# Channel mixing: the two groups of the first batch take turns feature by feature, in an order written out by hand

## The chip, the cores and the metric

The kernel runs on one core of one Trainium2 chip. TensorE does matrix products into PSUM (eight banks of 2 KB per partition), VectorE (DVE) and ScalarE (ACT) do the vector work, GpSimd (POOL) a little of it, SyncE (SP) issues the DMAs. The metric is the device time of one execution in microseconds.

## The reference, cut to what matters

Three layers follow each other on 4 batches of 768 positions and 384 channels.

```python
def _attn_ref(q, k, v, beta):                 # a recurrence over 768 positions, 4 batches x 8 heads
    ...
    return y                                  # gives x [4, 768, 384]

def _moe_ref(x, w_ch1, w_ch2):                # w_ch1 [384, 1536], w_ch2 [1536, 384]
    X = np.fft.fft(x, axis=1)
    X = np.fft.fft(X, axis=2)
    u = x + np.real(X)
    mu = np.mean(u, axis=-1, keepdims=True)
    var = np.mean((u - mu) ** 2, axis=-1, keepdims=True)
    un = (u - mu) / np.sqrt(var + 1e-06)
    return u + np.maximum(un @ w_ch1, 0.0) @ w_ch2

def _moe2_ref(x, w_in, w_spatial, b_spatial, w_out):
    ...                                       # a second mixer, over positions and channels
```

The change lies in `_moe_ref`, which is called channel mixing below.

## The kernel before

The recurrence is worked in chunks of 64 positions, batch by batch, and ends at about 316 us of the trace. While its last chunks run, batch 0 gets its Fourier transform and the normalised input of its first half is prepared. What follows is channel mixing, until 668 us, and then the second mixer.

**Groups and features.** Mixing takes the 3072 positions in eight groups of 384 (`for g in range(NG)`), two to a batch. The hidden layer of 1536 is cut into twelve features of 128. For a feature the first layer is nine products of 384 columns into one PSUM bank (L759: three chunks of the input times three passes, because each fp32 operand is split into a high and a low part). ScalarE takes the relu of that bank as the high part `hh` (L764), VectorE forms the low part `hl` (L765). The second layer is nine products into three accumulator banks `acc` (L774), which stay open over all twelve features; it runs one feature behind the first layer. At a group's end VectorE adds the three accumulators to x (L783).

**What stands beside the products.** Each of the 24 weight pieces (twelve of w_ch1, twelve of w_ch2) comes from DRAM as 8-byte numbers and is converted on the chip by `conv2`: one ScalarE pass (L677), three VectorE passes (L679, L680, L683), then the high part on ScalarE (L689) and the low part, the residual, on VectorE (L690). The first five pieces are converted ahead of mixing; the other 19 fall into it. The Fourier transform of batches 1 to 3 is `dft`: three vector steps on the rows (L575 to L586), one that combines them (L591 to L596), four first-stage pieces on TensorE (L603 to L609, copied out by L615), three second-stage pieces (L625, with L634 to L636) and an end that adds into x (L641 to L647). `mlp1_prep` prepares a group's input: statistics and reciprocal roots (L726 to L711), the normalised rows `un` (L731), and three chunks of three transposes each (L739), split into `uh` on ScalarE and `ul` on VectorE (L715, L716). Group 2 is the first of batch 1 and needs that batch's whole transform.

**Order and banks.** The recurrence is chained: `chain` makes each instruction stand behind the one before it on its engine, in the order of the code. In group 0 of mixing `behind` only keeps the instructions behind the recurrence; otherwise a scheduler, with a time model of its own, sets the order in mixing. Within the code `aside` hands out, one call a feature, conversions (in pairs), then transform steps, then the conversions of the last stage's weights. One PSUM pool holds the whole kernel: four X banks (first layer, transforms, transposes), three Y banks (accumulators) and one Z bank.

Of the kernel before, what the change touches and what calls it, by code (L numbers as in the profile page):

```python
# [33 lines left out]
PASS = ((0, 0), (0, 1), (1, 0))  # L34
# [4 lines left out]

CF = dict(
    skew=4, ring=20, kq=5, qt=3, mb=2, cvd=3, cve=2, kn=4, sv="hhhhhd", few=3,
    warm=20, keep=1, last=8, cuts=(0.5, 0.65), dfs=(1, 1, 1, 1, 2, 2, 3, 1, 1, 1, 2), cvt=(0, 0, 0, 0, 1, 1, 1, 1, 1, 1, 1), early=5, ahead=1,
)

BANKS = dict(X=4, Y=3, Z=1)
BANKS.update(pa="X", pz="Z", pb="Y", pc="Y", pd="Y", pf="X", h="X", o="Y", t="X")

# [6 lines left out]
WORD = [0] + [n for f in range(11) for n in (2 * f + 2, 2 * f + 1)] + [23]  # L56


class Kernel:
# [19 lines left out]
    def behind(self):  # L79
# [6 lines left out]
                self.tc.add_manual_dep(ins, last, dep, reason="issue order")  # L86
        self.seen = len(new)

    def load(self, out, in_):
        return self.nc.sync.dma_start(out=out, in_=in_)  # L90

    def bank(self, what, shape):
        tag = BANKS[what]
        t = self.ps.tile([128, 512], F32, name="bank" + tag, bufs=BANKS[tag])
# [472 lines left out]


    def dft(self, b, x, p):
        nc, sc, dc, sg = self.nc, self.sc, self.dc, self.sg  # L570
        X = x[b]
        ff = p(0, [128, 3, 388])
        for t in range(3):
            xs = p(3, [128, 2, DM])
            nc.vector.tensor_add(xs[:, 0], X[:, t], X[:, 3 + t])  # L575
            nc.vector.tensor_sub(xs[:, 1], X[:, t], X[:, 3 + t])
            f = p(6, [128, DM])
            nc.vector.tensor_copy(out=f[:, 0:193:192], in_=xs[:, 0, 0:193:192])
            nc.vector.tensor_add(f[:, 1:192], xs[:, 0, 1:192], xs[:, 0, 383:192:-1])
            nc.vector.tensor_sub(f[:, 193:384], xs[:, 1, 1:192], xs[:, 1, 383:192:-1])  # L580
            h = ff[:, t]
# [9 lines left out]
        nc.vector.tensor_add(sm, e1, e2)  # L591
        nc.vector.tensor_sub(e1, e1, e2)
        nc.vector.tensor_add(e2, e0, sm)
        nc.vector.scalar_tensor_tensor(out=r3, in0=e0, scalar=sg[:, 0:1], in1=e1, op0=MUL, op1=SUB)
        nc.vector.scalar_tensor_tensor(out=c15, in0=e0, scalar=sg[:, 1:2], in1=e1, op0=MUL, op1=ADD)
        nc.vector.scalar_tensor_tensor(out=e0, in0=e0, scalar=2.0, in1=sm, op0=MUL, op1=SUB)  # L596
# [119 lines left out]
        self.nc.vector.tensor_sub(lo, src, hi.bitcast(F32))  # L716


    def mlp1_prep(self, g, x, p):
        nc = self.nc  # L720
        assert g // 2 in self.mixed
        X = x[g // 2][:, g % 2 * 3 : g % 2 * 3 + 3]
        st = p.tile([128, 3, 6], F32, name="st1", bufs=2)
        mv = p.tile([128, 3, 2], F32, name="mv1", bufs=2)
        for t in range(3):
            nc.vector.bn_stats(out=st[:, t], in_=X[:, t])  # L726
            nc.vector.bn_aggr(out=mv[:, t], in_=st[:, t])
        r = self.rstd(p, mv, 3, "l1")
        un = p.tile([128, 3, DM], F32, name="un")
# [4 lines left out]
        u = [p.tile([128, 3, DM], F32R, name="u" + s, bufs=2) for s in "hl"]  # L734
        yield u
        for c in range(3):
            pt = self.bank("t", [128, DM])
            for t in range(3):
                nc.tensor.transpose(pt[:, t * 128 : t * 128 + 128], un[:, t, c * 128 : c * 128 + 128], self.idn)  # L739
            self.split(u[0][:, c], u[1][:, c], pt)  # L740
            yield u

    def mlp1(self, x, w1, w2, p, pu, cur, aside):
        nc = self.nc
        NG = NT // 3
        for g in range(NG):
# [3 lines left out]
            hs = {}  # L750
            for f in range(13):
                next(aside, None)
                if g == 0:
                    self.behind()
                if f < 12:
                    ph = self.bank("h", [128, DM])
                    for c in range(3):
                        for j, (i, k) in enumerate(PASS):
                            nc.tensor.matmul(  # L759
                                ph, lhsT=w1[f][i][:, c * 128 : c * 128 + 128], rhs=cur[k][:, c], start=(c + j == 0), stop=(c == 2 and j == 2)  # L760
                            )
                    hh = p.tile([128, DM], F32R, name="hh", bufs=3)
                    hl = p.tile([128, DM], F32R, name="hl", bufs=3)
                    nc.scalar.activation(hh, ph, AF.Relu)  # L764
                    nc.vector.scalar_tensor_tensor(  # L765
                        out=hl, in0=ph, scalar=0.0, in1=hh.bitcast(F32), op0=MAX, op1=SUB
                    )
                    hs[f] = (hh, hl)
                if f > 0:
                    e = f - 1  # L770
                    hx = hs.pop(e)
                    for t in range(3):
                        for j, (i, k) in enumerate(PASS):
                            nc.tensor.matmul(  # L774
                                acc[t],
                                lhsT=hx[i][:, t * 128 : t * 128 + 128],
                                rhs=w2[e][k],
                                start=(e == 0 and j == 0),
                                stop=(e == 11 and j == 2),
                            )  # L780
                if f in (5, 7, 9, 11):
                    new = next(gen, new)
            add = lambda t, xt: nc.vector.tensor_add(xt, acc[t], xt)  # L783
            sums = [(add, t, x[g // 2][:, g % 2 * 3 + t]) for t in range(3)]
            if g + 1 < NG:
                for f, *args in sums:
                    f(*args)
                sums = []
            cur = new
        for _ in aside:  # L790
            pass
        return sums


    def mlp2_prep(self, X, p):
# [102 lines left out]
    def run(self):  # L898
        nc, a = self.nc, self.a
        self.mixed, self.sc = set(), None  # L900
        c0, p0 = self.pool("keep")
        cps = self.tc.tile_pool(name="ps", bufs=1, space=PSUM)
        self.ps = cps.__enter__()
# [6 lines left out]
        e = {}  # L910
# [88 lines left out]

        sums = self.mlp1(x, [w[WORD.index(2 * f)] for f in range(12)], [w[WORD.index(2 * f + 1)] for f in range(12)], pm, e["u"], e["u0"], aside())  # L1000
        cm.__exit__(None, None, None)
        e["cu"].__exit__(None, None, None)
        cn, pn = self.pool("mlp2")
# [10 lines left out]
        cps.__exit__(None, None, None)  # L1014
        c0.__exit__(None, None, None)


# [107 lines left out]
```

## Time and profile before

| | us |
|---|---|
| median of three runs | 937.28 (937.04 to 937.43) |
| the profiled execution | 936.92 |
| its span, first to last instruction | 935.1 |
| TensorE busy | 884.8 (95%) |
| VectorE busy | 579.9 (62%) |
| ScalarE busy | 405.3 (43%) |
| GpSimd busy | 70.3 (8%) |

A profile is one execution of the program. Spans on TensorE have modelled ends, since products run into each other; a stream of products is read by the distance of their starts. [...] The chain of work that ended last is TensorE's for 72% of the span and VectorE's for 20%.

### The profile page before, as it was taken

How to read it: one execution, taken by the hardware profiler on the slowest of the kernel's cores; microseconds unless marked ns; L12 is line 12 of the kernel's file. 1: busy time of each engine (PE TensorE's matmuls, PEld its weight loads, DVE VectorE, ACT ScalarE, POOL GpSimd, SP SyncE). 2: the span in 40 equal slices, each digit the busy share in tenths (PEclk: the TensorE clock that was granted, in tenths of full speed). 3: DMA queues.
4: the chain of work that ended last, by engine and by line, in shares of the span. 5: the costliest groups of instructions: out<-in, count | busy, mean ns of one | idle time of the engine just before them, and what ended most of it. 6: DMA issues, size and time to landing. Idle time of an engine off the chain costs nothing.

```text
span 935.1 us, 18282 instructions
## 1 busy us (share of the span) xinstructions
PE 884.8 (95%) x7232; PEld 842.7 (90%) x7232; DVE 579.9 (62%) x1748; ACT 405.3 (43%) x1030; POOL 70.3 (8%) x75
## 2 busy tenths in 40 slices
PE   7969899999899769989999999999999999999998
PEld 7658888998898649989999999999999999899898
DVE  5999999998875899567479331322372442533521
ACT  2367878898966436222225111111261342332421
POOL 2000000000000000000000000000032132132221
PEclk8988999999999889999999999999999999999999
DMA  9676567643362530000150000000120000000001
GB/s 237 178 173 160 147 189 194 184 117 87 79 183 78 194 128 1 1 1 1 41 164 1 1 1 1 1 1 18 33 70 26 26 1 26 27 1 26 26 1 52
DMA packets 51160, 67.13 MB, mean 72 GB/s; under 512 B 28897, under 2 KB 41410, under 8 KB 51074
## 3 DMA queue, kind: packets, MB, share of 16 engines
q1 hardware_dynamic: 51074, 65.96, 24.9%
q8 instruction: 57, 0.93, 0.4%
q14 instruction: 29, 0.24, 0.1%
HBM read 61.22 MB, written 4.72 MB: 71 GB/s over the span
## 4 chain that ended last, share of the span: by engine, by line
PE 72%; DVE 20%; ACT 5%; issue 2%; DMA 1%; POOL 0%; ACTq 0%; DVEq 0%; POOLq 0%
PE bankX L759 14%; PE bankY L774 14%; PE bankX L867 11%; PE bankX L853 5%; PE bankX L828 5%; PE bankY L887 5%; DVE tm L273 4%; DVE Ts L278 4%; PE bankY L383 2%; PE bankY L367 2%; PE bankY L396 2%; PE bankY L398 2%; PE bankX L609 2%; PE bankX L198 1%; DVE cw L384 1%
## 5 line engine op out<-in xcount | busy, mean ns | idle before, releaser
L759 PE MATMUL bankX<-uh,w 128*128 128x384 f32 x576 | 163.9, 347 | 8.3 <-ACT w L689 4.7
L774 PE MATMUL bankY<-w,hh 128*128 128x384 f32 x576 | 136.6, 343 | 1.8 <-DVE w L690 1.5
L765 DVE SCALAR_TENSOR_TENSOR hl<-bankX,hh 128x384 fp32r<-128x384 f32 x96 | 52.7, 552 | 133.6 <-ACT hh L764 124.9
L764 ACT ACTIVATE hh<-bankX 128x384 fp32r<-128x384 f32 x96 | 46.8, 491 | 200.9 <-PE bankX L759 192.2
L759 PEld LDWEIGHTS bankX<-uh,w 128*128 128x128 f32 x576 | 106.5, 191 | 12.1 <-ACT w L689 6.4
L774 PEld LDWEIGHTS bankY<-w,hh 128*128 128x128 f32 x576 | 103.6, 190 | 4.2 <-DVE w L690 2.3
L867 PE MATMUL bankX<-ws,vh 128*128 128x384 f32 x384 | 98.9, 337 | 0.0
L759 PE MATMUL bankX<-ul,w 128*128 128x384 f32 x288 | 97.9, 340 | 0.0
L774 PE MATMUL bankY<-w,hl 128*128 128x384 f32 x288 | 82.2, 340 | 0.0
L875 DVE TENSOR_TENSOR g<-bankX,bsb 128x384 f32<-128x384 f32 x32 | 17.8, 558 | 103.6 <-PE bankX L867 103.6
L398 PE MATMUL bankY<-Sb,cw 112*112 112x96 f32 (+1 forms) x352 | 65.4, 269 | 11.4 <-DVE cw L384 9.2
L845 POOL TENSOR_TENSOR vl<-v,vh 128x512 fp32r<-128x512 f32 x24 | 31.7, 1328 | 531.0 <-DMA cvd<-in_ws_dram 457.4
L396 PE MATMUL bankY<-WU,gak 128*112 128x96 f32 (+1 forms) x384 | 69.3, 269 | 0.3
L867 PEld LDWEIGHTS bankX<-ws,vh 128*128 128x128 f32 x384 | 69.1, 188 | 0.0
L867 PE MATMUL bankX<-ws,vl 128*128 128x384 f32 x192 | 64.6, 337 | 0.0
L398 PEld LDWEIGHTS bankY<-Sb,cw 112*112 112x112 f32 (+1 forms) x352 | 49.1, 178 | 13.4 <-DVE cw L384 7.2
L278 DVE TENSOR_TENSOR Ts<-Ts,tm 128x110 f32<-128x110 f32 (+26 forms) x264 | 59.4, 263 | 0.8
L273 DVE TENSOR_TENSOR tm<-Ts 128x110 f32<-128x110 f32 (+26 forms) x264 | 59.3, 263 | 0.9
L367 PE MATMUL bankY<-gak,TT 128*128 128x96 f32 x384 | 53.4, 283 | 3.7 <-issue 2.7
L759 PEld LDWEIGHTS bankX<-ul,w 128*128 128x128 f32 x288 | 55.0, 191 | 0.0
L396 PEld LDWEIGHTS bankY<-WU,gak 128*112 128x112 f32 (+1 forms) x384 | 53.2, 181 | 1.2 <-ACT x L413 0.6
L774 PEld LDWEIGHTS bankY<-w,hl 128*128 128x128 f32 x288 | 53.2, 189 | 0.4 <-DVE hl L765 0.3
(166 smaller groups left out, 1787.3 us busy)
## 6 DMA issues: line engine op xcount, KB each, us to landing
kq<-in_kq_dram SPq DMA_DIRECT2D x40, 448.0 KB, 4.5
qt<-in_qt_dram SPq DMA_DIRECT2D x48, 196.0 KB, 3.8
gak<-in_kv_dram SPq DMA_DIRECT2D x48, 192.0 KB, 3.9
w<-in_w_dram SPq DMA_DIRECT2D x24, 384.0 KB, 7.0
out_dram<-ot SPq DMA_DIRECT2D x24, 192.0 KB, 2.0
kn<-in_kn_dram SPq DMA_DIRECT2D x16, 192.0 KB, 4.6
s<-in_wi_dram SPq DMA_DIRECT2D x6, 512.0 KB, 4.0
cvd<-in_ws_dram SPq DMA_DIRECT2D x12, 192.0 KB, 2.4
```

What stands on the lines that cost most here:

```text
L273: nc.vector.tensor_tensor(out=tm, in0=T[:, r, k : k + 1].to_broadcast(sh), in1=T[:, k : k + 1, :k].to_broadcast(sh), op=MUL)
L278: nc.vector.tensor_add(o, o, tm)
L367: nc.tensor.matmul(pb[:, hp].rearrange("p t d -> p (t d)"), lhsT=tt[:, o + hp], rhs=kv[:, hp], start=True, stop=True)
L396: nc.tensor.matmul(pd[:m, hp], lhsT=ak[:, hp, :m], rhs=u[:, hp], start=True, stop=(c == 0))
L398: nc.tensor.matmul(pd[:m, hp], lhsT=cw[:, hp, :m], rhs=sb[:, hp], start=False, stop=True)
L759: nc.tensor.matmul(ph, lhsT=w1[f][i][:, c * 128 : c * 128 + 128], rhs=cur[k][:, c], start=(c + j == 0), stop=(c == 2 and j == 2))
L764: nc.scalar.activation(hh, ph, AF.Relu)
L765: nc.vector.scalar_tensor_tensor(out=hl, in0=ph, scalar=0.0, in1=hh.bitcast(F32), op0=MAX, op1=SUB)
L774: nc.tensor.matmul(acc[t], lhsT=hx[i][:, t * 128 : t * 128 + 128], rhs=w2[e][k], start=(e == 0 and j == 0), stop=(e == 11 and j == 2),)
L828: nc.tensor.matmul(pv, lhsT=xT[t // 3][i][:, c, (t % 3) * 128 : (t % 3) * 128 + 128], rhs=wi[2 * c + 1][k], start=(c + j == 0), stop=(c == ...
L853: nc.tensor.matmul(pu, lhsT=wi[2 * c][i][:, f * 128 : f * 128 + 128], rhs=xT[hf][k][:, c], start=(c + j == 0), stop=(c == 2 and j == 2),)
L867: nc.tensor.matmul(pv, lhsT=vn[i][:, s, f * 128 : f * 128 + 128], rhs=ws[2 * s + hf][k], start=(s + j == 0), stop=(s == 5 and j == 2),)
```

## The change

Groups 0 and 1, the first batch, are worked together. A turn is one feature of one group: its first-layer products, what stands "between", then the second-layer products of that group's feature before. Group 0 starts, group 1 follows three features behind (`lag`), and then they alternate; turn n is counted through both groups: turns 0, 1 and 2 are group 0's features 0 to 2, turn 3 is group 1's feature 0, turn 4 group 0's feature 3 and so on to turn 25. Both groups read the same converted weights. For these turns the PSUM pool is closed and given out anew with two X banks, three Y and three V banks (group 1's accumulators), and afterwards again as before. Everything in these turns is chained in the order of the code: in each turn `beside` advances the last three weight conversions by one step each, and by tables `stats` and `turns` the preparation of groups 1 and 2 and the transform of batch 1 take their steps there. `dft` and `mlp1_prep` get places at which they can be split. From group 2 on the scheduler orders as before, and `aside` holds transforms 2 and 3 and then the last stage's weights. Group 1's `hh`, `hl` and group 2's input lie in another SBUF pool under the names `xh`, `xl`.

```diff
 CF = dict(
     ...
+    turns=(4, 5, 6, 7, 8, 9, 10, 11, 13, 14, 15, 16, 17, 17, 18, 19), stats=(((0, 1, 2, 3, 3), (2,)), ((20, 21, 22), (23, 24, 25))),
 )
 BANKS = dict(X=4, Y=3, Z=1)
+BANKS2 = dict(X=2, Y=3, V=3)
...
+    def psum(self, banks):
+        if self.ps:
+            self.cps.__exit__(None, None, None)
+        self.banks = banks
+        self.cps = self.tc.tile_pool(name="ps", bufs=1, space=PSUM, reuse_waits="tile")
+        self.ps = self.cps.__enter__()
...
-    def mlp1(self, x, w1, w2, p, pu, cur, aside):
+    def mlp1(self, x, w1, w2, p, pu, first, beside, aside):
...
+        def into(g, f, acc, cur, between=lambda: None):
+            if f < 12:
+                ph = self.bank("h", [128, DM])
+                ...
+                nc.scalar.activation(hh, ph, AF.Relu)
+                nc.vector.scalar_tensor_tensor(out=hl, in0=ph, scalar=0.0, in1=hh.bitcast(F32), op0=MAX, op1=SUB)
+                hs[g, f] = (hh, hl)
+            between()
+            if f > 0:
+                ...
+        self.psum(BANKS2)
+        accs = [[self.bank(n, [128, DM]) for _ in range(3)] for n in ("o", "o2")]
+        hx1 = [self.px.tile([128, 3, DM], F32R, name="x" + s, bufs=2) for s in "hl"]
+        lag, n = 3, 0
+        for s in range(13 + lag):
+            for g, f in ((1, s - lag), (0, s)):
+                if 0 <= f < 13:
+                    beside(n)
+                    into(g, f, accs[g], first[g], lambda: beside(n, True))
+                    if f == 12:
+                        for h, *args in sums(g, accs[g]):
+                            h(*args)
+                    self.chain()
+                    n += 1
+        self.psum(BANKS)
+        cur = first[2]
+        for g in range(2, NG):
...
+        def beside(n, between=False):
+            for g, (stats, turned) in enumerate(CF["stats"]):
+                for _ in range((turned if between else stats).count(n)):
+                    first[1 + g] = next(preps[g])
+            if between:
+                for _ in range(CF["turns"].count(n)):
+                    next(mx)
+                return
+            if len(gens) < 24 - CF["early"]:
+                gens.append(self.conv2(e["u"], w[CF["early"] + len(gens)]))
+            for g in gens[:-4:-1]:
+                next(g, None)
...
         def aside():
-            for i in range(CF["early"], 24):
-                self.conv(e["u"], w[i])
-                if i - CF["early"] >= CF["ahead"] and i % 2:
-                    yield
-            n = 0
-            while next(mx, 1) != 1:
-                n += 1
-                if not 4 < n <= 12 or n % 2 == 0:
+            for i, _ in enumerate(mx):
+                yield
+                if i % 12 < 4:
                     yield
```

Up to the first product of mixing the order on every engine is the same before and now, and in the second mixer too. Two places show what moves.

TensorE at the start of group 0, before: `uh` and `ul` are the parts of the normalised input, `w_F` the converted piece of feature F, `idn` the unit matrix of the transposes.

```order
L739 MATMUL bankX<-idn,un 128x128 x6
L759 MATMUL bankX<-uh,w_0_4306 128x384
L759 MATMUL bankX<-ul,w_0_4306 128x384
L759 MATMUL bankX<-uh,w_0_4306 128x384
L759 MATMUL bankX<-uh,w_1_4355 128x384
L759 MATMUL bankX<-ul,w_1_4355 128x384
L759 MATMUL bankX<-uh,w_1_4355 128x384
L759 MATMUL bankX<-uh,w_0_4306 128x384
L759 MATMUL bankX<-uh,w_1_4355 128x384
```

The same place now (the lines of the new file are 776 for the first layer, 792 for the second):

```order
L761 MATMUL bankX<-idn,un 128x128 x6
L776 MATMUL bankX<-uh,w_0_4306 128x384
L776 MATMUL bankX<-ul,w_0_4306 128x384
L776 MATMUL bankX<-uh,w_0_4306 128x384 x2
L776 MATMUL bankX<-ul,w_0_4306 128x384
L776 MATMUL bankX<-uh,w_0_4306 128x384 x2
L776 MATMUL bankX<-ul,w_0_4306 128x384
L776 MATMUL bankX<-uh,w_0_4306 128x384
L776 MATMUL bankX<-uh,w_1_4355 128x384
L776 MATMUL bankX<-ul,w_1_4355 128x384
L776 MATMUL bankX<-uh,w_1_4355 128x384 x2
```

The first chunk of features 0 and 1 came first, the other chunks as the input arrived; now feature 0 is complete before feature 1 begins.

VectorE a few features into group 0, before: `cve` and `cvd` are the buffers of a conversion, `s_` tiles those of the transform, `l1r`, `l1v` the roots of group 1's preparation, `x_62` is batch 1.

```order
L575 TENSOR_TENSOR s_4979<-x_62 128x384
L765 SCALAR_TENSOR_TENSOR hl<-bankX,hh 128x384
L576 TENSOR_TENSOR s_4979<-x_62 128x384
L683 SCALAR_TENSOR_TENSOR cvd<-w_3_4497,cvd 128x384
L679 TENSOR_SCALAR cve<-w_4_4501 128x384
L683 SCALAR_TENSOR_TENSOR cvd<-w_2_4499,cvd 128x384
L679 TENSOR_SCALAR cve<-w_3_4503 128x384
L707 RECIPROCAL l1r<-l1s 128x3
L578 COPY s_4982<-s_4979 128x2
L579 TENSOR_TENSOR s_4982<-s_4979 128x191
L580 TENSOR_TENSOR s_4982<-s_4979 128x191
L680 SCALAR_TENSOR_TENSOR cvd<-cvd,cve 128x384
```

Now, from the `hl` of turn 6 to that of turn 7 (`xl` is group 1's `hl`):

```order
L784 SCALAR_TENSOR_TENSOR hl<-bankX,hh 128x384
L587 TENSOR_TENSOR s_4786<-x_62 128x384
L588 TENSOR_TENSOR s_4786<-x_62 128x384
L590 COPY s_4789<-s_4786 128x2
L591 TENSOR_TENSOR s_4789<-s_4786 128x191
L592 TENSOR_TENSOR s_4789<-s_4786 128x191
L695 TENSOR_SCALAR cve<-w_6_4509 128x384
L696 SCALAR_TENSOR_TENSOR cvd<-cvd,cve 128x384
L699 SCALAR_TENSOR_TENSOR cvd<-w_6_4509,cvd 128x384
L706 TENSOR_TENSOR w_4_4808<-cvd,w_4_4808 128x384
L784 SCALAR_TENSOR_TENSOR xl<-bankX,xh 128x384
```

The steps of two conversions, a transform and a preparation were interleaved one by one; now a turn holds half a transform step, one conversion's three passes, the residual of the conversion before, and the turn's `hl`, each in one piece.

## Rows read from the trace of the kernel before

**Rows 1.** Busy time by stretches: us, engines' busy time (instructions), PEclk, DMA share, GB/s.

```profile
320.00:370.00 50.00, 39.89 (x190) 33.89 (x189) 50.00 (x141) 23.20 (x50) 0.00 (x0) 0.90 0.30 117
340.00:350.00 10.00, 5.19 (x22) 3.85 (x21) 10.00 (x25) 3.05 (x6) 0.00 (x0) 0.89 0.01 2
350.00:360.00 10.00, 10.00 (x48) 9.65 (x47) 10.00 (x24) 5.38 (x13) 0.00 (x0) 0.77 0.00 0
410.00:668.00 258.00, 258.00 (x1552) 256.41 (x1553) 111.31 (x274) 60.69 (x131) 0.00 (x0) 1.00 0.07 23
```

**Rows 2.** Groups, TensorE, 316.3 to 412 us: busy, mean ns | idle before, releasers.

```profile
L759 PE MATMUL bankX<-uh,w 128*128 128x384 f32 x126 | 38.7, 369 | 8.3 <-ACT w L689 4.7 <-DVE w L690 3.6
L774 PE MATMUL bankY<-w,hh 128*128 128x384 f32 x120 | 32.1, 359 | 1.8 <-DVE w L690 1.5 <-ACT w L689 0.2
L759 PE MATMUL bankX<-ul,w 128*128 128x384 f32 x63 | 22.3, 354 | 0.0
L774 PE MATMUL bankY<-w,hl 128*128 128x384 f32 x60 | 18.4, 346 | 0.0
...
L739 PE MATMUL bankX<-idn,un 128*128 128x128 f32 x12 | 2.4, 301 | 2.4 <-DVE un L731 2.4
```

**Rows 3.** Chain of waits, 380 to 530 us: start, length, what.

```profile
383.92 1.76 PE bankX L625 x16
...
519.76 4.35 PE bankX L759 x25
```

**Rows 4.** TensorE in order of time: start, length, engine, line, operation [idle before].

```profile
327.14 0.51 PE L759 MATMUL bankX<-uh,w 128*128 128x384 f32 x1 [1.85 <-ACT w L689]
...
368.41 0.49 PE L739 MATMUL bankX<-idn,un 128*128 128x128 f32 x3
368.73 0.30 PE L603 MATMUL bankX<-s,s 128*97 128x65 f32 x2
...
369.87 0.42 PE L774 MATMUL bankY<-w,hh 128*128 128x384 f32 x1
```

**Rows 5.** All engines in order of time, 316 to 318 us.

```profile
316.35 0.67 PE L759 MATMUL bankX<-uh,w 128*128 128x384 f32 x1
...
316.68 1.13 DVE L716 TENSOR_TENSOR ul<-bankX,uh 128x384 fp32r<-128x384 f32 x2 [1.68 <-ACT uh L715]
...
317.73 0.55 DVE L690 TENSOR_TENSOR w<-cvd,w 128x384 fp32r<-128x384 f32 x1
```

**Rows 6.** VectorE in order of time, 302 to 310.5 us.

```profile
302.60 0.54 DVE L690 TENSOR_TENSOR w<-cvd,w 128x384 fp32r<-128x384 f32 x1
303.06 0.34 DVE L679 TENSOR_SCALAR cve<-w 128x384 int32<-128x384 int32 x1
...
304.51 0.35 DVE L357 TENSOR_TENSOR gak<-gak,n_all 128x192 f32<-128x192 f32 x1
...
305.31 0.55 DVE L726 BATCH_NORM_STATS2 st<-x 128x6 f32<-128x384 f32 x1
...
308.89 1.26 DVE L731 TENSOR_SCALAR un<-x,mv,l1r 128x384 f32<-128x384 f32 x3
310.07 0.55 DVE L690 TENSOR_TENSOR w<-cvd,w 128x384 fp32r<-128x384 f32 x1
```

**Rows 7.** Groups of the whole execution: busy, mean ns | idle before, releaser.

```profile
L765 DVE SCALAR_TENSOR_TENSOR hl<-bankX,hh 128x384 fp32r<-128x384 f32 x96 | 52.7, 552 | 133.6 <-ACT hh L764 124.9
L764 ACT ACTIVATE hh<-bankX 128x384 fp32r<-128x384 f32 x96 | 46.8, 491 | 200.9 <-PE bankX L759 192.2
```

**Rows 8.** VectorE in order of time, 268 to 280 us: batch 0's transform steps.

```profile
268.28 0.56 DVE L575 TENSOR_TENSOR s<-x 128x384 f32<-128x384 f32 x1
...
270.70 0.35 DVE L357 TENSOR_TENSOR gak<-gak,n_all 128x192 f32<-128x192 f32 x1
...
276.56 0.56 DVE L591 TENSOR_TENSOR s<-s 128x384 f32<-128x384 f32 x1
...
279.88 0.35 DVE L357 TENSOR_TENSOR gak<-gak,n_all 128x192 f32<-128x192 f32 x1
```

More of the change, by code (lines that the diff above doesn't have):

```diff
@@ L43 @@
     skew=4, ring=20, kq=5, qt=3, mb=2, cvd=3, cve=2, kn=4, sv="hhhhhd", few=3,
-    warm=20, keep=1, last=8, cuts=(0.5, 0.65), dfs=(1, 1, 1, 1, 2, 2, 3, 1, 1, 1, 2), cvt=(0, 0, 0, 0, 1, 1, 1, 1, 1, 1, 1), early=5, ahead=1,
+    warm=20, keep=1, last=8, cuts=(0.5, 0.65), dfs=(1, 1, 1, 1, 2, 2, 3, 1, 1, 1, 2), cvt=(0, 0, 0, 0, 1, 1, 1, 1, 1, 1, 1), early=5,
+    turns=(4, 5, 6, 7, 8, 9, 10, 11, 13, 14, 15, 16, 17, 17, 18, 19), stats=(((0, 1, 2, 3, 3), (2,)), ((20, 21, 22), (23, 24, 25))),
 )
 BANKS = dict(X=4, Y=3, Z=1)
-BANKS.update(pa="X", pz="Z", pb="Y", pc="Y", pd="Y", pf="X", h="X", o="Y", t="X")
+BANKS2 = dict(X=2, Y=3, V=3)
+USE = dict(pa="X", pz="Z", pb="Y", pc="Y", pd="Y", pf="X", h="X", o="Y", o2="V", t="X")
 SEQ = [bc[1:] for bc in sorted((c + CF["skew"] * b, b, c) for b in range(B) for c in range(NC))]
@@ L92, in bank @@
     def bank(self, what, shape):
-        tag = BANKS[what]
-        t = self.ps.tile([128, 512], F32, name="bank" + tag, bufs=BANKS[tag])
+        tag = USE[what]
+        t = self.ps.tile([128, 512], F32, name="bank" + tag, bufs=self.banks[tag])
         n = int(np.prod(shape[1:]))
@@ L580, in dft @@
             nc.vector.tensor_sub(f[:, 193:384], xs[:, 1, 1:192], xs[:, 1, 383:192:-1])
+            if b == 1:
+                yield
             h = ff[:, t]
@@ L593, in dft @@
         nc.vector.tensor_add(e2, e0, sm)
+        if b == 1:
+            yield
         nc.vector.scalar_tensor_tensor(out=r3, in0=e0, scalar=sg[:, 0:1], in1=e1, op0=MUL, op1=SUB)
@@ L727, in mlp1_prep @@
             nc.vector.bn_aggr(out=mv[:, t], in_=st[:, t])
+        if fine:
+            yield
         r = self.rstd(p, mv, 3, "l1")
+        if fine:
+            yield
         un = p.tile([128, 3, DM], F32, name="un")
@@ L733, in mlp1_prep @@
             )
-        u = [p.tile([128, 3, DM], F32R, name="u" + s, bufs=2) for s in "hl"]
+        u = [p.tile([128, 3, DM], F32R, name="u" + s, bufs=2) if g != 2 else self.px.tile([128, 3, DM], F32R, name="x" + s, bufs=2) for s in "hl"]
         yield u
@@ L741, in mlp1_prep, with sums @@
             yield u
-    def mlp1(self, x, w1, w2, p, pu, cur, aside):
+    def mlp1(self, x, w1, w2, p, pu, first, beside, aside):
         nc = self.nc
         NG = NT // 3
-        for g in range(NG):
+        hs = {}
+        def into(g, f, acc, cur, between=lambda: None):
+            if f < 12:
+                ph = self.bank("h", [128, DM])
+                for c in range(3):
+                    for j, (i, k) in enumerate(PASS):
+                        nc.tensor.matmul(
+                            ph, lhsT=w1[f][i][:, c * 128 : c * 128 + 128], rhs=cur[k][:, c], start=(c + j == 0), stop=(c == 2 and j == 2)
+                        )
+                if g == 1:
+                    hh, hl = (t[:, f % 3] for t in hx1)
+                else:
+                    hh, hl = (p.tile([128, DM], F32R, name="h" + s, bufs=3) for s in "hl")
+                nc.scalar.activation(hh, ph, AF.Relu)
[3 more added lines that the diff above has]
+            if f > 0:
+                e = f - 1
+                hx = hs.pop((g, e))
+                for t in range(3):
+                    for j, (i, k) in enumerate(PASS):
+                        nc.tensor.matmul(
+                            acc[t],
+                            lhsT=hx[i][:, t * 128 : t * 128 + 128],
+                            rhs=w2[e][k],
+                            start=(e == 0 and j == 0),
+                            stop=(e == 11 and j == 2),
+                        )
+        def sums(g, acc):
+            add = lambda t, xt: nc.vector.tensor_add(xt, acc[t], xt)
+            return [(add, t, x[g // 2][:, g % 2 * 3 + t]) for t in range(3)]
+        self.psum(BANKS2)
[15 more added lines that the diff above has]
+        for g in range(2, NG):
@@ L749, in mlp1 @@
             acc = [self.bank("o", [128, DM]) for _ in range(3)]
-            hs = {}
             for f in range(13):
                 next(aside, None)
-                if g == 0:
+                if g == 2:
                     self.behind()
[L755 to L780, printed above, removed]
+                into(g, f, acc, cur)
                 if f in (5, 7, 9, 11):
                     new = next(gen, new)
-            add = lambda t, xt: nc.vector.tensor_add(xt, acc[t], xt)
-            sums = [(add, t, x[g // 2][:, g % 2 * 3 + t]) for t in range(3)]
             if g + 1 < NG:
-                for f, *args in sums:
+                for f, *args in sums(g, acc):
                     f(*args)
-                sums = []
             cur = new
@@ L791, in mlp1 @@
             pass
-        return sums
+        return sums(NG - 1, acc)
     def mlp2_prep(self, X, p):
@@ L901, in run @@
         c0, p0 = self.pool("keep")
-        cps = self.tc.tile_pool(name="ps", bufs=1, space=PSUM)
-        self.ps = cps.__enter__()
+        self.ps = None
+        self.psum(BANKS)
         x = [p0.tile([128, 6, DM], F32, name=f"x{b}") for b in range(B)]
@@ L982, in run @@
         mx = mix()
-        def aside():
-            for i in range(CF["early"], 24):
-                self.conv(e["u"], w[i])
-                if i - CF["early"] >= CF["ahead"] and i % 2:
-                    yield
-            n = 0
-            while next(mx, 1) != 1:
-                n += 1
-                if not 4 < n <= 12 or n % 2 == 0:
+        first = {0: e["u0"]}
+        gens, preps = [], [self.mlp1_prep(g, x, e["u"], True) for g in (1, 2)]
+        def beside(n, between=False):
[10 more added lines that the diff above has]
+                next(g, None)
+        def aside():
+            for i, _ in enumerate(mx):
+                yield
+                if i % 12 < 4:
                     yield
@@ L998, in aside @@
                         yield
-        sums = self.mlp1(x, [w[WORD.index(2 * f)] for f in range(12)], [w[WORD.index(2 * f + 1)] for f in range(12)], pm, e["u"], e["u0"], aside())
+        sums = self.mlp1(x, [w[WORD.index(2 * f)] for f in range(12)], [w[WORD.index(2 * f + 1)] for f in range(12)], pm, e["u"], first, beside, aside())
         cm.__exit__(None, None, None)
```

4 lines of the change are left out of this document (2 added, 2 removed).

## The prediction, on record before the result was known

> **What bounds the kernel now.** I read the page's slices first, then the table by stretches of time, the groups of instructions on TensorE, the chain of waits and, in order of time, what TensorE and VectorE do from 268 to 412 us. The slices send the reader to one place: behind the recurrent stage TensorE is dense except at the start of channel mixing. From 320 to 370 us VectorE is busy 50.00 of 50 us and TensorE 39.89; from 410 to 668 us TensorE is busy 258.00 of 258 us at a granted clock of 1.00 [rows 1]. So mixing is bound by VectorE for its first 50 us and by TensorE afterwards, and only the first part can be shortened. VectorE is full there because group 0 needs a new converted weight piece every 1.6 us of TensorE work while the vector work of batch 1's Fourier transform and group 1's preparation run on the same engine. TensorE's waits between 316 and 412 us are 8.3 and 1.8 us for conversions (the releasers are the two lines that write w) and 2.4 us for group 2's normalised input [rows 2].
>
> How far before gets: by 412 us it has issued 126 + 63 first-layer and 120 + 60 second-layer products, 369 in all [rows 2]. Groups 0 and 1 have 2 x 12 x 18 = 432. Of the 12 transposes in the same rows nine are group 1's, and three are group 2's first chunk, which needs batch 1's whole transform; so that is done. 25 products in a row take 4.35 us [rows 3], 0.174 each; 63 more take 11.0, and the other two chunks of group 2 at 0.32 [rows 4] 0.6. As TensorE never rests again, before has groups 0 and 1, transform 1 and group 2's input behind it at 412 + 11.6 = **423.6 us**. The change is priced by the same mark.
>
> **The part up to 316.35 us** is the same instructions in the same order on every engine, the last stage too; nothing is taken or lost there.
>
> **The change, step by step, to that mark.** No product, conversion or transform step is dropped. TensorE's own work from 316.35 us on: 432 x 0.174 = 75.2; four first-stage pieces of the transform at 1.14 (368.73 to 369.87 in [rows 4]) and three second-stage pieces at 0.88 (16 products take 1.76, eight a piece [rows 3]) with 0.2 for the last row: 7.4; six chunks of transposes at 0.32: 1.9. Together 84.5, which alone would end at 400.9.
>
> To it come waits.
> (a) The start. Before, three features' first products are interleaved and begin at 316.35 with the first chunk of the input. Now feature 0 goes whole, into a bank of the pool given out anew; it stands behind the last of the residuals ul, which is the row of two at 316.68; the next instruction starts at 317.73 [rows 5], and the last result is 0.1 later. I take 1.5 us. Bounds: 0, if the pool gives another bank, to 1.5.
> (b) The clock. [...] Bounds 0 to 3.
> (c) Group 1's input. VectorE from 317.73: residual of a piece 0.46, statistics and roots 3.58 (305.31 to 308.89), three normalisations 1.18, two conversions at 1.45 (303.06 to 304.51), one more residual 0.46 and three relu residuals hl at 0.46 (as 302.60 to 303.06) [rows 6]: 9.96. Inside stands a wait of 0.9, since hl of feature 0 needs the first product, over at 320.7, and its relu of 491 ns [rows 7]. So hl of feature 2 ends at 328.6. With two banks chunk 2 of the transposes waits for it, chunk 3 for the first ul; each chunk goes on through ScalarE and VectorE for about a microsecond. Group 1's first product starts near 330.4. TensorE's own work to there is over at 320.7 + 4 x 1.57 + 3 x 0.32 = 327.9: 2.5 us of waiting. Bounds 1 to 4.
> (d) The turns. TensorE needs 18 x 0.174 = 3.13 a turn. VectorE needs a conversion 1.45, the residual of the one before 0.46 and hl 0.46: 2.37. ScalarE has a relu and two conversion passes, each about as long as the relu's 491 ns [rows 7], half a turn: it is not late. A transform step of turn n stands behind that turn's hl, so turns 5 to 12 carry them: three pairs of half steps at 2.42 (268.28 to 270.70), then two at 3.32 together (276.56 to 279.88) [rows 8]. 8 x 2.37 + 3 x 2.42 + 3.32 = 29.5 against 8 x 3.13 = 25.0: here VectorE is the bound again. TensorE starts turn 5 at 330.4 + 1.57 + 3.13 = 335.1 (turn 3 has one product only), VectorE its share at 330.9 + 2 x 2.37 = 335.6. The first transform product, in turn 13, needs hl of turn 12: VectorE has it at 335.6 + 29.5 = 365.1, TensorE would want it at 335.1 + 25.0 + 1.6 = 361.7. So TensorE loses **3.4** over turns 8 to 13, in pieces under 1.5 us. Bounds 1 to 7. From turn 13 on TensorE has 3.13 + 1.14 and VectorE 2.37, and the debt is paid.
> (e) Two transform pieces in turn 17: the second needs the bank of that turn's relu, 491 + 552 ns [rows 7] behind its product, and the first covers 0.88: with hand-overs 0.4. The statistics of group 2 in turns 20 to 22 (about 6.5 us of VectorE) lie beside two and a half turns, 8 us, and cost nothing; where that cover fails they cost 1.
>
> Mark: 400.9 + 1.5 + 1.3 + 2.5 + 3.4 + 0.4 = **410.0**, 13.6 earlier than 423.6.
>
> I take 2 us off. One and a half for a further fall of the clock: before, after stop-and-go from 340 to 350 us (TensorE busy 5.19 of 10), the next 10 us show TensorE busy throughout at a mean clock of 0.77 [rows 1], so 4.6 us of them at the lower level, which costs 2.3; step (c) has less idle time, so two thirds of that. A half for groups 2 and 3, where the scheduler's order puts transforms 2 and 3 ahead: VectorE's work in front of hl of feature 4 ends within 0.2 us of TensorE's need. SyncE's weight loads keep their order, and each conversion comes no earlier than before, so no DMA becomes late. The last stage's weights are converted about a group and a half later than before, during groups 4 and 5; they are first read behind group 7, so some 80 us of products still cover them.
>
> 13.6 - 2.0 = 11.6. The profiled execution took 936.92 us (span 935.1, 1.8 around it), 0.36 under the median of 937.28 that is forecast: **925.7 us**.
>
> [...]
>
> **Rivals.**
> 1. [...] 5%.
> 2. No change: queues in hand order add half a microsecond to every turn, because hl must wait for ScalarE's relu, which stands behind a conversion's two passes, and the next bank hangs on hl. 23 turns x 0.5 = 11.5: 937. Against it: at 1.04 us relu and hl [rows 7] fit into the 1.57 of the second product. 5%.
> 3. Half given back: groups 2 and 3 wait on VectorE as group 0 did, for half of the 10.1 us of [rows 2]: 931. Against it: no conversions are left there, and before is full from 410 on. 15%.
> 4. More than forecast: the bank at the start is free, the clock rises at once and hand-overs overlap, so (a), (b) and the 2 us fall away: 921. 15%.
>
> Forecast: 60%, 923 to 929. Range for 8 in 10: **920.5 to 933**. Faster by over 0.2% (what a measurement of this kernel can tell): 0.90; within 0.2% 0.05; slower 0.05.
>
> **What would show it.** Steps (a) and (b): a gap of about 1.5 us ahead of the first mixing product and a clock near 0.5 behind it. (c): TensorE idle some 2.5 us between 325 and 331. (d): VectorE full and TensorE 85 to 90% busy from 345 to 366, waits named for the residual of w and for hl. The mark: group 2's first product near 410. Wrong would be: a clock below 0.9 from 340 on, waits of TensorE in most turns behind 13, or idle time after 412.

## The result and the profile after

The changed kernel takes **923.34 us** (median of 4 runs, 922.73 to 924.39), the kernel before in the same rounds 937.36 (937.04 to 937.82): a ratio of 0.9856, 95% interval 0.9843 to 0.9868. Forecast were 925.7 us and a range of 920.5 to 933. The profiled execution took 922.85 us, with a span of 921.0 against 935.1.

The table by stretches of the kernel after, in the columns of [rows 1]:

```profile
core 0: us, PE busy (x) PEld busy (x) DVE busy (x) ACT busy (x) POOL busy (x), PEclk, DMA share, GB/s
320.00:370.00 50.00, 46.24 (x267) 43.74 (x266) 46.99 (x119) 21.79 (x49) 0.00 (x0) 1.00 0.28 111
410.00:655.00 245.00, 245.00 (x1479) 243.47 (x1478) 117.96 (x316) 58.88 (x127) 0.00 (x0) 1.00 0.08 24
```

From 320 to 370 us TensorE is now busy 46.24 us (before 39.89), and its clock (PEclk, the granted one as a share of the full speed) is 1.00 throughout (before 0.90). VectorE is still nearly full, 46.99 of 50. From 410 us on TensorE is full, as before. What is left of TensorE's waits, by what is waited for (us in all, times, the longest), from 316 to 420 us:

```profile
PE bankX L776 <- DVE ul L732: 2.4, 2, 1.7
PE bankX L619 <- DVE hl L784: 1.3, 1, 1.3
PE bankY L792 <- DVE w L706: 1.1, 2, 0.6
PE bankX L761 <- DVE hl L784: 0.5, 1, 0.5
PE bankX L641 <- DVE xl L784: 0.3, 1, 0.3
```

5.6 us stand where [rows 2] had 12.5. Each is a wait that the prediction named; the places of five of them, and of the mark, in the timeline of TensorE:

```profile
316.69 0.44 PE L776 MATMUL bankX<-uh,w 128*128 128x384 f32 x1 [1.73 <-DVE ul L732]
328.27 0.44 PE L776 MATMUL bankX<-uh,w 128*128 128x384 f32 x1 [0.69 <-DVE ul L732]
351.27 0.44 PE L792 MATMUL bankY<-w,hh 128*128 128x384 f32 x1 [0.49 <-DVE w L706]
358.45 0.44 PE L792 MATMUL bankY<-w,hh 128*128 128x384 f32 x1 [0.59 <-DVE w L706]
362.97 0.38 PE L619 MATMUL bankX<-s,s 128*97 128x65 f32 x2 [1.28 <-DVE hl L784]
...
409.17 0.44 PE L776 MATMUL bankX<-xh,w 128*128 128x384 f32 x1
```

These are the first mixing product, group 1's first, the second products of turns 10 and 12, the first transform product of turn 13, and the mark (group 2's first product, forecast 410.0). From the mark to the end are 921.0 - 409.17 = 511.8 us; before, 935.1 - 423.6 = 511.5. So 0.3 us at most was given back behind the mark, and the mark before is itself an estimate.

The shorter waits are only half of the gain. The same stretches of TensorE, before from the first mixing product to 412 us, and after from the first mixing product to the mark:

```profile
316.35:412.00 95.65, 83.16 (x461) 76.50 (x460) 81.87 (x239) 33.55 (x74) 0.00 (x0) 0.94 0.19 74
```

```profile
316.69:409.17 92.48, 88.38 (x526) 84.85 (x526) 76.28 (x191) 33.77 (x77) 0.00 (x0) 1.00 0.19 74
```

To its mark the kernel before was busy 83.2 us and by the prediction's count 11.6 more, 94.8 in all; now the same work takes 88.4. The 6.4 us between them are mostly the clock: a mean of 0.94 over 95.65 us means 11.5 us at 0.50, the clock that before shows from 350 to 354 us; they cost up to half of that, 5.7 us (an estimate from this row). Now TensorE waits less and its clock is 1.00 throughout.

### The profile page after: what moved, and what is told of

It reads as the page before. It is cut to its first block, busy times and chain, and to the rows that moved or that the text cites. A ratio compares the mean times of both kernels' runs of the same rounds, so it can differ in the third digit from the quotient of the medians.

```text
span 921.0 us, 18253 instructions
## 1 busy us (share of the span) xinstructions
PE 874.2 (95%) x7232; PEld 835.9 (91%) x7232; DVE 584.5 (63%) x1748; ACT 404.3 (44%) x1030; POOL 70.3 (8%) x75
## 4 chain that ended last, share of the span: by engine, by line
PE 73%; DVE 20%; ACT 4%; issue 1%; DMA 1%; POOL 0%; ACTq 0%; DVEq 0%; SPq 0%; POOLq 0%
PE bankX L776 14%; PE bankY L792 13%; PE bankX L914 11%; PE bankX L900 5%; PE bankX L875 5%; PE bankY L934 5%; DVE tm L284 4%; DVE Ts L289 4%; PE bankY L394 2%; PE bankY L409 2%; PE bankY L378 2%; PE bankY L407 2%; PE bankX L625 2%; PE bankV L792 1%; PE bankX L209 1%
## 5 line engine op out<-in xcount | busy, mean ns | idle before, releaser
L776 PE MATMUL bankX<-uh,w 128*128 128x384 f32 x504 | 141.2, 340 | 2.4 <-DVE ul L732 2.4
L792 PE MATMUL bankY<-w,hh 128*128 128x384 f32 x504 | 117.5, 339 | 1.1 <-DVE w L706 1.1
L784 DVE SCALAR_TENSOR_TENSOR hl<-bankX,hh 128x384 fp32r<-128x384 f32 x84 | 46.4, 555 | 109.1 <-ACT hh L783 104.7
L783 ACT ACTIVATE hh<-bankX 128x384 fp32r<-128x384 f32 x84 | 41.0, 491 | 158.7 <-PE bankX L776 152.8
L776 PEld LDWEIGHTS bankX<-uh,w 128*128 128x128 f32 x504 | 92.3, 188 | 3.1 <-DVE ul L732 2.9
L792 PEld LDWEIGHTS bankY<-w,hh 128*128 128x128 f32 x504 | 89.9, 188 | 2.0 <-DVE w L706 1.7
L776 PE MATMUL bankX<-ul,w 128*128 128x384 f32 x252 | 84.9, 337 | 0.0
L792 PE MATMUL bankY<-w,hl 128*128 128x384 f32 x252 | 71.9, 338 | 0.0
L378 PEld LDWEIGHTS bankY<-gak,TT 128*128 128x128 f32 x384 | 47.4, 194 | 5.5 <-issue 3.0
L394 PE MATMUL bankY<-gak,WU 128*112 128x112 f32 x352 | 44.9, 272 | 6.2 <-ACT WU L383 4.6
```

The source lines that it names most:

```text
L378: nc.tensor.matmul(pb[:, hp].rearrange("p t d -> p (t d)"), lhsT=tt[:, o + hp], rhs=kv[:, hp], start=True, stop=True)
L394: nc.tensor.matmul(pc[:, hp], lhsT=w[:, hp], rhs=gas[bc][:, hp, : C + D], start=True, stop=True)
L776: nc.tensor.matmul(ph, lhsT=w1[f][i][:, c * 128 : c * 128 + 128], rhs=cur[k][:, c], start=(c + j == 0), stop=(c == 2 and j == 2))
L784: nc.vector.scalar_tensor_tensor(out=hl, in0=ph, scalar=0.0, in1=hh.bitcast(F32), op0=MAX, op1=SUB)
L792: nc.tensor.matmul(acc[t], lhsT=hx[i][:, t * 128 : t * 128 + 128], rhs=w2[e][k], start=(e == 0 and j == 0), stop=(e == 11 and j == 2),)
```

## Two executions of one program

The changed kernel ran again beside three of the experiments (the first bank, the half steps on GpSimd, and both).

> The changed kernel itself, on the chip and in the rounds of the three kernels that follow, so that tenths of a per cent can be told. Every theory: 923.3 us, within 0.7.

Measured: 922.91 us median (922.59 to 925.33, 4 runs), ratio to before 0.985 (0.9834 to 0.9867). The profiled execution was its longest, 925.33 us, and by chance shows what the prediction had assumed. Stretches of it, and then two of the same stretches of the first profile:

```profile
305.00:310.00 5.00, 3.04 (x27) 2.88 (x28) 4.42 (x16) 2.26 (x7) 0.00 (x0) 1.00 0.27 75
310.00:315.00 5.00, 4.17 (x26) 3.56 (x24) 4.86 (x11) 1.73 (x4) 0.00 (x0) 0.54 0.02 7
315.00:320.00 5.00, 3.84 (x15) 3.24 (x14) 3.24 (x9) 2.70 (x6) 0.00 (x0) 0.50 0.74 249
320.00:325.00 5.00, 5.00 (x20) 5.00 (x20) 3.04 (x12) 2.07 (x5) 0.00 (x0) 0.60 0.98 375
```

```profile
305.00:310.00 5.00, 4.99 (x26) 5.00 (x26) 4.42 (x16) 1.88 (x5) 0.00 (x0) 0.50 0.02 3
310.00:315.00 5.00, 4.20 (x33) 3.52 (x32) 4.86 (x11) 2.78 (x7) 0.00 (x0) 0.88 0.29 79
```

From 300 us on the clock falls to 0.50 once in both, at the sparse end of the recurrent stage, but not at the same place. TensorE rests 2.67 us ahead of the same eight products, which take 1.99 us in the first profile and 1.10 in this one:

```profile
305.01 1.99 PE L378 MATMUL bankY<-gak,TT 128*128 128x96 f32 x8 [2.67 <-issue]
```

```profile
305.00 1.10 PE L378 MATMUL bankY<-gak,TT 128*128 128x96 f32 x8 [2.67 <-issue]
```

In the first profile the clock has fallen there and is up again by 312 us, on work that waits for other engines anyway. In this one it falls only near 310 us, behind a second rest of 1.95 us, and stays low until about 324, through the first eighteen mixing products; the profile before also shows it low at the first of them, which takes 0.67 us to its end [rows 5], at a clock of 0.50 from 316 to 317 us. So this execution is the one to hold against the prediction, step by step:

| start of, us | predicted | this execution | first profile |
|---|---|---|---|
| the first mixing product | 317.9 | 317.91 | 316.69 |
| group 1's first product | 330.4 | 330.88 | 328.27 |
| the first transform product | 365.1 | 365.56 | 362.97 |
| group 2's first product | 410.0 | 411.81 | 409.17 |
| the end of the span | 923.5 | 923.6 | 921.0 |

```profile
317.91 0.69 PE L776 MATMUL bankX<-uh,w 128*128 128x384 f32 x1 [1.16 <-DVE ul L732]
...
330.88 0.44 PE L776 MATMUL bankX<-uh,w 128*128 128x384 f32 x1 [0.70 <-DVE ul L732]
...
365.56 0.38 PE L619 MATMUL bankX<-s,s 128*97 128x65 f32 x2 [1.28 <-DVE hl L784]
...
411.81 0.45 PE L776 MATMUL bankX<-xh,w 128*128 128x384 f32 x1
```

Three of its four runs were at 922.6 to 923.0. That these three had the early fall is likely but not shown: they have no profile, and their mean clocks (0.978, 0.984, 0.984) do not settle it.

The place of the fall is not something that the change is shown to set. With a late fall on both sides, this execution and the profiled one before, the gain is 936.92 - 925.33 = 11.6 us; the rest of the 14 us between the medians goes with the early fall. Whether the kernel before would gain by an early fall, no run shows.

## Experiments: what makes the gain

My theory was that the gain comes from the turns: one converted piece serves two groups, so TensorE asks for one per 3.1 us instead of 1.6. The rival was that the hand-written order gives it and the turns are not needed. Two runs took one away each.

**Order without turns:**

```diff
-        lag, n = 3, 0
+        lag, n = 13, 0
...
-            if len(gens) < 24 - CF["early"]:
-                gens.append(self.conv2(e["u"], w[CF["early"] + len(gens)]))
-            for g in gens[:-4:-1]:
-                next(g, None)
+            for _ in range(2):
+                (the same, twice a turn)
```

> The hand-written order, the banks and the half steps of the transform are kept, but group 1 begins only when group 0 is through (its distance is 13 features instead of 3), and each turn of group 0 begins a second conversion, so that a weight piece is there every half turn as one group alone needs it. If the gain comes from the two groups sharing the conversions (my theory), it is lost: 13 turns of 3.13 us (41 us of TensorE) meet 19 conversions and their residuals (36), 12 relu residuals (6), group 1's input (6) and the transform's steps (11), 59 us of VectorE; TensorE waits 10 to 18 us before 380 us, its clock falls below 0.95 there, and the time is 934 to 945 us. If the hand-written order is what gives the gain, the time stays within 923 to 928 us.

Measured: 939.9 us (937.7 to 940.67), ratio 1.0033 (1.0021 to 1.0046). The whole gain is gone. From 320 to 370 us TensorE is busy 36.50 us at a clock of 0.93, and its waits from 316 to 400 us are those of a group that outruns its relu, the relu's residual and group 1's input:

```profile
PE bankY L792 <- ACT hh L783: 5.4, 4, 1.8
PE bankY L792 <- DVE hl L784: 3.9, 7, 1.3
PE bankX L761 <- DVE un L752: 3.0, 1, 3.0
```

No wait of TensorE names a conversion here. ScalarE's relu stands behind conversion passes, and in the same stretch these wait for VectorE's residuals:

```profile
ACT cvd L693 <- DVE w L706: 22.2, 15, 3.0
```

This is one order without turns, with two conversions a turn in one piece; that no other could gain is not shown.

**Turns without order:**

```diff
                     if f == 12:
                         ...
-                    self.chain()
+                    self.behind()
```

> The two groups take turns as in the changed kernel, but inside the turns the scheduler chooses the order again (only each turn is held behind the work before it, as before the change). If the turns give the gain (my theory), most of it stays: 922 to 929 us. If the hand-written order does, it goes: 933 to 938 us, with waits of TensorE for conversions of 5 us and more between 320 and 380 us.

Measured: 945.25 us (944.91 to 946.17), ratio 1.009 (1.0075 to 1.0105): slower than before. Both theories fall as they stood: neither half, as built here, gains alone. The timeline of VectorE in this run shows why. These are the small steps of group 1's roots and its normalisation:

```profile
323.33 0.17 DVE L721 TENSOR_SCALAR l1v<-mv 128x3 f32<-128x3 f32 x1
...
337.35 0.18 DVE L727 RECIPROCAL l1r<-l1v 128x3 f32<-128x3 f32 x1
339.42 1.26 DVE L752 TENSOR_SCALAR un<-x,mv,l1r 128x384 f32<-128x384 f32 x3
```

and in the changed kernel:

```profile
319.63 0.16 DVE L721 TENSOR_SCALAR l1v<-mv 128x3 f32<-128x3 f32 x1
...
322.86 1.25 DVE L752 TENSOR_SCALAR un<-x,mv,l1r 128x384 f32<-128x384 f32 x3
```

VectorE is busy 10.00 of 10 us from 320 to 360 in that run, but largely on conversions and transform steps put between the links of the one short chain that TensorE awaits. From the first of these rows to `un` it needs 16.1 us, in the changed kernel 3.2. TensorE pays with this:

```profile
339.96 1.54 PE L761 MATMUL bankX<-idn,un 128*128 128x128 f32 x6 [8.28 <-DVE un L752]
```

and with a clock of 0.51 and 0.50 in the two slices from 330 to 350 us. (In the profiles of this run and of the one with one X bank, mixing also began 1.3 us later than in the first profile, at 317.9 and 318.0 us; the recurrent stage, which these edits leave alone, has that delay from about 150 us on.)

**Order for the first eight turns only:**

```diff
-                    self.chain()
+                    (self.chain if n < 8 else self.behind)()
```

> The turns, with the hand-written order in the first eight turns alone (until group 1's input is through) and the scheduler's order in the other eighteen. If the free order lost its 22 us at the place where group 1's input came 16 us late, nearly all of it is back: 923 to 926 us. If the free order also costs in the later turns (transforms 2 and 3 taken up early, and waits of TensorE again near 420 us, as the run with free order showed 3.6 us there), 926 to 932 us.

Measured: 926.39 us (925.99 to 929.04), ratio 0.9895 (0.9882 to 0.9909). So 18.9 of the 22.3 us between the free order and the order in full (945.25 to 922.91) lie in the first eight turns. The other 3.5 come late, in the way of rival 3 of the prediction: VectorE is then full from 390 to 410 us, and the transposes of group 2's input wait for a relu residual (the waits of step (d), in turns 10 to 13, are gone in this run):

```profile
PE bankX L761 <- DVE xl L784: 2.8, 1, 2.8
```

**One X bank instead of two:**

```diff
-BANKS2 = dict(X=2, Y=3, V=3)
+BANKS2 = dict(X=1, Y=3, V=3)
```

> One bank instead of two for the first-layer products, the transposes and the transform pieces during the turns. My theory: relu and its residual (1.04 us) fit beside the second product of a turn (1.57 us), so the turns without other users of the bank lose nothing; turns 13 to 19, where a transform piece takes the bank too, lose about a microsecond each, and the start of group 1 one or two: 928 to 934 us, clock above 0.95. [...]

Measured: 950.23 us (948.67 to 950.48), ratio 1.0138 (1.0123 to 1.0153). My size was far off. Waits like these stand ahead of every transform piece and of two of the three chunks of group 2's transposes:

```profile
373.86 0.38 PE L619 MATMUL bankX<-s,s 128*97 128x65 f32 x2 [1.17 <-DVE xl L784]
```

1.17 us is a relu and its residual with hand-overs. TensorE's waits of 0.3 us and more add up to 24 us between 316 and 440, against 5.6 in the changed kernel: 18.5 of the 27 us. I had priced the pieces at about one a turn and left out the first products of ordinary turns (6.6 us of the 24), which also wait when `hl` stands behind a late conversion. The clock, in stretches of this run:

```profile
330.00:340.00 10.00, 6.50 (x24) 5.52 (x23) 5.38 (x11) 3.13 (x7) 0.00 (x0) 0.68 0.54 208
350.00:360.00 10.00, 9.04 (x50) 8.37 (x49) 9.79 (x30) 4.27 (x9) 0.00 (x0) 1.00 0.00 1
370.00:380.00 10.00, 7.05 (x45) 6.18 (x44) 6.08 (x14) 3.26 (x7) 0.00 (x0) 1.00 0.00 0
...
390.00:400.00 10.00, 6.49 (x42) 6.01 (x42) 3.68 (x8) 2.63 (x6) 0.00 (x0) 0.93 0.01 2
400.00:410.00 10.00, 8.83 (x41) 8.51 (x41) 3.93 (x10) 2.40 (x6) 0.00 (x0) 0.73 0.00 0
```

Waits of about a microsecond every few, with TensorE busy as little as 7.05 of 10, left the clock at 1.00 from 350 to 390 us. It did fall at two places: to 0.68 from 330 to 340, amid four waits of 1.2 to 1.7 us within 11 us, and to 0.73 from 400 to 410, behind ten microseconds with 6.49 busy. The second bank is worth 27 us, mostly as waits; what the two falls add was not separated.

## Experiments: the waits that are left

**Step (a), the first bank:**

```diff
+        ready = [self.bank("h", [128, DM])]
         accs = [[self.bank(n, [128, DM]) for _ in range(3)] for n in ("o", "o2")]
...
-                ph = self.bank("h", [128, DM])
+                ph = ready.pop() if ready else self.bank("h", [128, DM])
```

> The first product's bank is given out ahead of the accumulators, so that it is one that no transpose of group 0's input still holds; the first mixing product then waits for ScalarE's uh instead of VectorE's last residual. By step (a) of the prediction alone, its wait of 1.73 us goes and the time falls by 1.7, to 921.6. My theory now: VectorE's chain to group 1's input sets the next point and gains at most its own wait for the first relu; TensorE waits longer ahead of the transposes of group 1 instead. 0.2 to 0.9 us less than the changed kernel: 922.4 to 923.1.

Measured: 922.21 us (921.89 to 922.49), 0.7 under the changed kernel beside it; ratio to before 0.9844 (0.9829 to 0.9858). The wait of 1.7 at the start is gone, and a new one stands ahead of group 1's first transposes:

```profile
PE bankX L761 <- DVE un L752: 0.6, 1, 0.6
```

As expected: where VectorE sets the next point, TensorE arrives earlier and waits there.

**Step (d), relief of VectorE by GpSimd:** batch 1's half steps are issued there.

```diff
+        ve = nc.gpsimd if b == 1 else nc.vector
...
-            nc.vector.tensor_add(xs[:, 0], X[:, t], X[:, 3 + t])
+            ve.tensor_add(xs[:, 0], X[:, t], X[:, 3 + t])
             ... (and so for all ten instructions of a pair)
```

> The six half steps of batch 1's transform (sums and differences of turns 4 to 9) go from VectorE to GpSimd, which is idle there. Theory: VectorE's debt of step (d) goes, so the waits ahead of turns 11, 12 and 13 (0.49, 0.59 and 1.28 us) go: 2.0 to 2.4 us less than the changed kernel, 921 us. GpSimd, at 1.01 us for a 128x384 difference, needs about 4.5 us for a pair of half steps and has 6.3. Rival: the two engines hinder each other; VectorE's 128x384 operations grow from 0.55 us, and the time is 923 to 926 us.

Measured: 926.26 us (925.86 to 927.18), ratio 0.9888 (0.9874 to 0.9903); slower than the changed kernel. The waits in turns 10 to 13 did vanish (TensorE busy 20.00 of 20 from 350 to 370 us). But nothing held GpSimd back: it ran ahead, from 274 to 277 us and from 304 to 319, beside the end of the recurrent stage, and group 0's three normalisations on VectorE took 2.17 us instead of 1.26. Mixing began 6.0 us later than in the first profile (322.73 against 316.69), and the vanished waits won only a part of that back.

**Both edits:**

> Both of these edits. If VectorE bounds everything up to turn 13, relieving it lets part of the start's 1.7 us through: 919.5 to 921 us. If GpSimd hinders VectorE: no faster than the run with the first bank alone.

Measured: 924.78 us (924.67 to 926.58), ratio 0.9876 (0.9861 to 0.9891): the late start again (320.25 against 314.23 with the first bank alone).

**GpSimd held back:** the edit before the last, and

```diff
+            if b == 1:
+                ve.tensor_copy(out=xs[:, 0, 0:2], in_=self.hold[:, 0:2].bitcast(F32))
```

where `hold` is the turn's relu residual.

> The six half steps on GpSimd as before, but each pair begins behind that turn's relu residual, through a copy of two of its columns, so that they run in turns 4 to 10 and not ahead of mixing. Theory: VectorE is slowed only beside GpSimd's 14 us; if by a half (0.56 to 0.83 us, as seen ahead of mixing), that is under 5 us against the 7.3 us taken from it, so the waits ahead of turns 11 to 13 (2.4 us) go and the start is as in the changed kernel: 920.5 to 922 us. If the slowing eats the whole relief: 922.5 to 925 us, with the waits still there.

Measured: 923.32 us (923.19 to 923.45), ratio 0.9857 (0.9843 to 0.987): no gain; the waits stand as they were (0.6 and 0.9 us for w, 1.4 in turn 13). VectorE beside GpSimd, and one of the GpSimd instructions of that time:

```profile
334.28 1.25 DVE L702 SCALAR_TENSOR_TENSOR cvd<-w,cvd 128x384 int32<-128x384 int32 x1
335.45 1.37 DVE L709 TENSOR_TENSOR w<-cvd,w 128x384 fp32r<-128x384 f32 x1
336.74 0.55 DVE L787 SCALAR_TENSOR_TENSOR xl<-bankX,xh 128x384 fp32r<-128x384 f32 x1
...
341.43 1.25 DVE L702 SCALAR_TENSOR_TENSOR cvd<-w,cvd 128x384 int32<-128x384 int32 x1
```

```profile
333.78 1.34 POOL L590 TENSOR_TENSOR s<-x 128x384 f32<-128x384 f32 x1
```

The same two turns in the changed kernel, with the half steps on VectorE:

```profile
336.06 0.56 DVE L699 SCALAR_TENSOR_TENSOR cvd<-w,cvd 128x384 int32<-128x384 int32 x1
...
343.13 0.56 DVE L699 SCALAR_TENSOR_TENSOR cvd<-w,cvd 128x384 int32<-128x384 int32 x1
```

The conversion's residual takes 1.37 us instead of 0.55 while GpSimd works through its 128x384 sums; the relu residual, with one operand in PSUM, stays at 0.55. Two turns take VectorE 341.43 - 334.28 = 7.15 us; with the half steps on VectorE itself they take 343.13 - 336.06 = 7.07. What was moved came back in full. Only operations without a PSUM operand were slowed in these turns. In these turns the two engines together did no more than VectorE alone.

**The half steps spread** (with the first bank of above):

```diff
-    turns=(4, 5, 6, 7, 8, 9, 10, 11, 13, 14, 15, 16, 17, 17, 18, 19)
+    turns=(4, 5, 6, 8, 9, 11, 12, 14, 15, 16, 17, 17, 18, 18, 19, 19)
```

> The first bank given out early, and the transform's steps spread over more turns (half steps in turns 4 to 14 with turns free of them between, the pieces in turns 15 to 19, two a turn from 17 on). VectorE's debt has ten turns with 0.76 us of slack instead of eight: the waits of step (d) fall from 2.4 us to under 0.8; three more turns with two pieces cost 0.3 each as turn 17 did. Theory: 920.0 to 921.6 us. If VectorE's debt isn't what the waits ahead of turns 11 to 13 are: no change from 922.2, or more with the double pieces.

Measured: **920.56 us** (920.13 to 921.02, 5 runs), ratio to before 0.9829 (0.9815 to 0.9842): the best of all, 2.4 under the changed kernel and 1.65 under the run with the first bank alone. Every wait of TensorE from 314 to 420 us that is left:

```profile
PE bankX L776 <- DVE ul L732: 0.7, 1, 0.7
PE bankX L761 <- DVE un L752: 0.6, 1, 0.6
PE bankX L761 <- DVE hl L784: 0.5, 1, 0.5
PE bankX L641 <- DVE hl L784: 0.3, 1, 0.3
PE bankX L641 <- DVE xl L784: 0.3, 1, 0.3
PE bankY L792 <- DVE hl L784: 0.3, 1, 0.3
```

The waits of step (d) are gone, so they were VectorE's debt; of the two waits on L641 (0.3 each) one is new, from the turns that hold two pieces.

## Why the prediction was right, and where it was not

The mechanism and the places were right: waits at the start, at group 1's input, in turns 10 to 13 (the second products of turns 10 and 12, which the later expectations count as ahead of 11 and 12, and the transform product of turn 13) and in turn 17, TensorE full behind them, at most 0.3 us given back. The forecast missed the median by 2.4 us, inside the likeliest case's own 923 to 929. By its steps, first profile and second execution:

- **(a)** The first product 1.5 us later than before's 316.35: measured 0.34 and 1.56. The cause, the last residual `ul`, is named by the wait ahead of that product (1.73 and 1.16) and shown by the run with the first bank; its worth by itself is only 0.7 us.
- **(b)** 1.3 us of low clock, a term that no run shows. In the first profile no mixing product ran at the low clock (it is 1.00 from 316 us on). In the second a clock of 0.50 covered eighteen products, and they took 5.9 us instead of 3.3: 2.6. This term sets the forecast apart from the first profile: the prediction took as given that the clock is low when mixing begins, which one execution of before shows (0.50 from 312 to 317 us), and the place of the low stretch varies between executions.
- **(c)** 2.5 us of waiting: measured 0.47 + 0.69, and 0.70. The first product of group 1 came at 328.27 and 330.88 against a forecast of 330.4.
- **(d)** 3.4 us: measured 0.49 + 0.59 + 1.28 = 2.4, and 2.4 again. **(e)** 0.4: measured 0.31 in both.
- **TensorE's own work** was sized too small. Between its first mixing product and the mark in the first profile TensorE was busy 88.4 of 92.5 us, where I had 84.5. I took every product at 0.174 us and every hand-over to a transform piece or a transpose at nothing; 364.19 to 409.17 shows two products in 0.43 instead of 0.35 behind each of them, about a microsecond in all. Some of the busy time is also a wait: three transposes of group 1's first chunk span 0.86 us at 323.39, since their weight loads wait for the rows `un` one by one (0.9 us in three waits); three of group 2's, at 407.06, take 0.24. The rest of the 3.9 is not accounted for. This 3.9 too little met 5 too much in the start, the waits and the clock, so that the mark, 410.0 against 409.17, is better than its terms.
- **The 2 us taken off.** No further fall of the clock came: it is 1.00 from 330 us on in both executions. (The fall of before that the prediction reasons from reads 0.50 from 350 to 354 us and 0.83 in the next two.) Behind the mark 0.3 us was given back in both (511.8 against 511.5). The run with eight ordered turns shows that more lies near: there a wait of 2.8 us stands at group 2's input.
- **The end of the second execution**, 923.6 against a forecast of 923.5, is luck to that extent: its mark came 1.8 us late, and of the 2 us taken off only 0.3 was lost behind it.
- **The hand-over of order** was under-rated. The prediction spoke of the order as the means by which the steps come late or early, but put no price on its absence; with the turns it is 22 us, more than the whole gain.

The slower time, to which the prediction gave 5%, did not come: the clock of the changed kernel is 1.00 from 330 us on. In the run with one bank, with four times its waits (24 us against 5.6), it was 1.00 from 350 to 390 us and fell at two places, to 0.68 and 0.73. Rival 2's half microsecond a turn is not there: no wait stands between turns but those named. Of what rival 4 (921) let fall away, the first profile bears out (b) and most of (a) and of the 2 us, but not the free bank, and the larger own work took the rest.

Open is what puts the fall of the clock before or behind 310 us in one execution or another; the program up to there is the same.

## What to carry to other kernels

In this kernel, halving the demand on the engine that is late helped only where that engine worked first on what others await: sharing the conversions and ordering them, as built here, were each worth nothing alone, and 12 to 14 us together. Nearly half of that is, by the estimate above, not waits but a higher granted clock (1.00 against a mean of 0.94). A wait taken away where the next engine in the chain is full came back mostly as waits at the next points (0.7 of 1.7 us was kept); spreading that engine's work over turns that have slack gave more, 1.65 us. GpSimd was no relief for VectorE while both read two SBUF operands: two turns took VectorE 7.15 us with its help and 7.07 without.

## What the runs showed of the hardware

A VectorE operation with two SBUF operands went from 0.55 to 1.37 us beside GpSimd's 128x384 sums, one with a PSUM operand stayed at 0.55, and GpSimd's own sums went from 0.99 (where it ran ahead) to 1.34 us. And one program shows a stretch at a clock of 0.50, behind the same rest of 2.67 us, at 305 to 311 us in one execution and at 310 to 324 in another; the spans differ by 2.6 us (923.6 against 921.0).
